# Second row slab's statistics moved to ScalarE, three row slabs loaded ahead of the weights, and the first feed-forward tiles cut into other column widths

## The chip, the cores and the metric

The kernel runs on one core of a Trainium2 chip. The metric is device time in microseconds (us), as a median over runs. Everything that is said of single instructions comes from one profiled execution, which has its own time. TensorE appears in the profile as PE (its weight loads as PEld), VectorE as DVE, ScalarE as ACT, GpSimd as POOL, and the queue that issues the DMAs as SP.

## The reference

`x` is 2048 x 640 in bf16. It is layer-normed, and the result `xn` goes two ways: through a spectral filter (2-D FFT, product with a complex weight, inverse FFT) and through a gated feed-forward network whose output is passed through SiLU. The output is `x + s * g`.

```python
def _layernorm(x, axis=-1, eps=1e-5):
    m = jnp.mean(x, axis=axis, keepdims=True)
    v = jnp.var(x, axis=axis, keepdims=True)
    return (x - m) / jnp.sqrt(v + eps)
...
    def _A_ref(x, w_r, w_i):            # w_r, w_i: 2048 x 321
        X = rfft2(x.astype(jnp.float32)) * (w_r + 1j * w_i)
        return irfft2(X, s=(S, D)).astype(jnp.bfloat16)

    def _B_ref(x, w_gate, w_up, w_down):  # 640 x 1536 twice, 1536 x 640
        return (_gelu(x @ w_gate) * (x @ w_up)) @ w_down

    xn = _layernorm(A_x, axis=-1)
    s = _A_ref(xn, A_w_r, A_w_i)
    g = _silu(_B_ref(xn, B_w_gate, B_w_up, B_w_down))
    return x + s * g
```

## The kernel before, in words

The 2048 rows are dealt into 16 slabs of 128 rows (one row per partition); slab n1 lies in `X[:, n1, :]`. Four slabs make a group g, so a group has 512 columns once it is transposed. The feed-forward network works on groups: the normed slabs are transposed into `xnT[g]` (five chunks of 128 features by 512 rows), and for each of the 12 tiles t of 128 hidden features there is a gate piece and an up piece. A piece (`ffn_piece`, five matmuls, one per chunk) goes into a PSUM bank of its kind: `psg` for gates and `psu` for ups, two banks each, used in turn. A gate is taken out of its bank by a Gelu on ACT into a tile `ge`; an up is taken out by a multiplication with `ge` on DVE into `uT`. After the 12 tiles the product with `w_down` follows (`down_third`). The Fourier stages run as matmuls between these pieces.

Layer norm of a slab takes four steps. `half_stats` (line 174) takes `bn_stats` of each half of the row on DVE, and `bn_aggr` (line 179) joins them to mean and variance. `root` adds epsilon on DVE (line 188) and raises to the power -0.5 on POOL (line 190). `norm` (line 196) subtracts and scales in place on DVE; `norm_parts` does so in two column parts, of 384 and 256 features, so that the first transposes can start sooner. `slab_Tparts` (lines 726 to 730) transposes the two parts on PE and copies each out of PSUM; for slab 0 both copies are on ACT, for slab 1 the second is on DVE. `slab_T` (lines 469 to 473) does a whole slab, with the copy on ACT for slab 2 and on DVE for slab 3.

The order of the work is written out by hand. Every engine takes its instructions in the order of the program. The list `back` holds the feed-forward work, entry by entry, and `plan[s]` holds what is issued behind entry s (`put`). Entries 0 to 2 compute tiles 0 to 2 on slab 0 and then on slab 1, with pieces of 128 columns (`ffn_slab`). Entries 3 to 7 compute tiles 3 to 7 on slabs 0 and 1 together, with 256 columns (`ffn_part` with h = 0), and entries 8 to 15 tiles 0 to 7 on slabs 2 and 3 (h = 1). From entry 16 on pieces have 512 columns (`ffn_half`). Before `back` starts, PE runs warm-up matmuls on constants (`warm_pe`, line 512).

The loads are issued on SP at the very beginning (lines 94 to 108) and are served in this order: slab 0, the gate weights of tiles 0 to 2, slab 1, the up weights of tile 0, those of tiles 1 and 2, slabs 2 and 3 together, then gate and up weights of tiles 3 and 4, of 5 and 6, of 7, and later slabs and weights.

POOL makes integer tables for the Fourier matrices: `vt_iota` (line 221) writes half a table each, and `tinv_phase` (line 308) and `ft_phase` (lines 338 to 342) work on them. `inv_rest` is five tiny DVE instructions on constants; `ft_v` (line 333) is a table row on ACT, one behind each of ten entries.

Of the kernel before, what the change touches and what calls it, by code (L numbers as in the profile page):

```python
# [9 lines left out]
FP32 = mybir.dt.float32  # L10
# [4 lines left out]
P = 128  # L15
# [61 lines left out]
def build(nc, env):  # L77
# [5 lines left out]
    def load_x(n0, n, eng=nc.sync):  # L83
        eng.dma_start(out=X[:, n0:n0 + n, :], in_=xv[:, n0:n0 + n, :])
# [6 lines left out]
        for k in range(2):  # L91
            load_w(k, t0, t1)

    load_x(0, 1)
    load_w(0, 0, 3)
    load_x(1, 1)
    load_w(1, 0, 1)
    load_w(1, 1, 3)
    load_x(2, 2)
    load_gu(3, 5)  # L100
    load_gu(5, 7)
    load_gu(7, 8)
# [82 lines left out]
    def root(n0, n):  # L185
# [6 lines left out]
        for k in range(n):  # L192
            rstd[n0 + k] = r[:, k:k + 1]

    def norm(n1, c0=0, c1_=D):
        nc.vector.tensor_scalar(out=X[:, n1, c0:c1_], in0=X[:, n1, c0:c1_], scalar1=mva[n1 // 4][:, n1 % 4, 0:1],
                                scalar2=rstd[n1], op0=ALU.subtract, op1=ALU.mult)
        if c1_ == D:
            done.add(("n", n1))
# [15 lines left out]
    lint = gtile([LH], INT32)  # L215
    nc.gpsimd.iota(lint, pattern=[[1, LH]], base=0, channel_multiplier=0)
    vt = gtile([NS, P], INT32)

    def vt_iota(h):
        nc.vector.memset(vt[:, 8 * h, 0:1], 0)  # L220
# [80 lines left out]
    vt_iota(0)  # L301
    stats(0)
    root(0, 1)
    inv_consts()

    def tinv_phase(h):
# [356 lines left out]
    def ffn_piece(g, t, k, c0, c1_):  # L663
        new_uT(g)
        for j in range(c0 // P, c1_ // P):
            assert ("T", 4 * g + j) in done
        ps = bank(k)[:, c0:c1_]
        WT = (Wg, Wu)[k]
        for c in range(5):
            nc.tensor.matmul(ps, lhsT=WT[:, c, t * P:(t + 1) * P], rhs=xnT[g][:, c, c0:c1_],  # L670
                             start=(c == 0), stop=(c == 4))
        if k == 0:
            ges[t] = work.tile([P, 512], BF16, tag="ge", bufs=3, name="ge")[:, c0:c1_]
            nc.scalar.activation(out=ges[t], in_=ps, func=ACT.Gelu_apprx_tanh)  # L674
        else:
            nc.vector.tensor_tensor(out=uT[g][:, t, c0:c1_], in0=ps, in1=ges[t], op=ALU.mult)  # L676

    def ffn_part(g, t, h):
        for k in range(2):
# [28 lines left out]
        for t, k in tk:  # L708
            ffn_piece(0, t, k, j * P, j * P + P)

    GG, REST = ((0, 0), (1, 0)), ((0, 1), (2, 0))

    def run(*items):
        for it in items:
# [8 lines left out]
    def slab_Tparts(n1):  # L723
        if n1 == 0:
            xnT[0] = xg.tile([P, 5, 512], BF16, tag="xg", name="xnT0")
        for (a, b), ev in zip(PARTS, (nc.scalar.copy, nc.scalar.copy if n1 == 0 else nc.vector.tensor_copy)):
            pt = psB.tile([P, 5, P], BF16, tag="b")
            for c in range(a, b):
                nc.tensor.transpose(out=pt[:, c, :], in_=X[:, n1, c * P:(c + 1) * P], identity=ident)
            ev(out=xnT[0][:, a:b, n1 * P:n1 * P + P], in_=pt[:, a:b, :])  # L730
        done.add(("T", n1))

    NP = 8
    back = [(run, (ffn_slab, 0, GG), (norm_parts, 1), (vt_iota, 1), (ffn_slab, 0, REST), (slab_Tparts, 1),
             (ffn_slab, 0, ((1, 1), (2, 1))),
             (half_stats, 2, 0)),
            (run, (ffn_slab, 1, GG + REST[:1]), (half_stats, 2, 1), (root, 2, 1), (ffn_slab, 1, REST[1:])),
            (run, (ffn_slab, 1, ((1, 1), (2, 1))), (norm, 2), (stats, 3), (root, 3, 1))]
    for h in range(2):
        for t in range(0 if h else 3, NP):  # L740
            back.append((ffn_part, 0, t, h))
    for g in range(4):
        for t in range(NP if g == 0 else 0, NT):
            for k in range(2):
# [6 lines left out]
    def put(s, *item):  # L751
        plan[s].append(item)

    put(5, norm, 3)
    put(5, slab_T, 2, 1)
    put(6, slab_T, 3, 0)
    for g in range(5):
        put(3 + g, ft_v, g)
        put(8 + g, ft_v, 5 + g)
# [92 lines left out]

    warm_pe(19)
    norm_parts(0)
    stats(1)
    slab_Tparts(0)
    warm_pe(2)
    root(1, 1)
    inv_rest()

    put(5, phase_const)

    for s, b in enumerate(back):
# [34 lines left out]
```

## Time and profile before

| | us |
|---|---|
| median of 3 runs | 207.86 (207.09 to 207.91) |
| profiled execution | 207.12 |
| its span, first to last instruction | 205.3 |
| PE busy in the span | 198.7 (97%) |
| DVE busy | 129.9 (63%) |
| ACT busy | 124.7 (61%) |
| POOL busy | 33.9 (17%) |

The time of the profiled execution is its span and 1.82 us around it. PE is busy nearly throughout, so what counts is the time in which PE has nothing to do and the time that its matmuls take. A matmul's record goes on for a while after the next one has begun, since matmuls are pipelined: the distance between the starts of two pieces tells how long PE needs for one. These distances are 0.28 us for five matmuls of 128 columns, 0.545 us for 256 and 1.08 us for 512 (starts at 9.71 and 9.99, 12.20 and 12.75, 32.67 and 33.75 us). The part of the span that the change touches lies before 27 us.

### The profile page before, as it was taken

To read this page: it belongs to the slowest core of one execution; us is meant where nothing else is said; L and a number is where in the kernel's file an instruction comes from. 1 tells how busy PE (TensorE), PEld (TensorE's weight loads), DVE (VectorE), ACT (ScalarE), POOL (GpSimd) and SP (SyncE) were. 2 spreads that over 40 slices of the span, in tenths; PEclk is the share of its full clock that TensorE was granted. 3 is DMA by queue.
4 is the path that set the end of the run, shared out by engine and by line. 5 is a ranking of instruction groups with operands and counts; after the bars stand their busy time and mean duration, and the time that the engine had idled before them with its cause. 6 is when DMAs were issued, how large, how long until landed. Compare 5 with 4: busy or idle time off the path is not lost.

```text
span 205.3 us, 4412 instructions
## 1 busy us (share of the span) xinstructions
PE 198.7 (97%) x1626; PEld 121.2 (59%) x1643; DVE 129.9 (63%) x357; ACT 124.7 (61%) x230; POOL 33.9 (17%) x61
## 2 busy tenths in 40 slices
PE   7999999999999999999999999999999999999993
PEld 5788855777555555475644444447775555556762
DVE  7886966797678842336565655433568768775653
ACT  2547567767868787225787777424555654656641
POOL 5328688945001100000000000000000000000000
PEclk9999999999999999999999999999999999999998
DMA  5999999899987799289965332369731332242111
GB/s 168 303 305 314 369 291 135 168 146 179 176 161 169 166 186 172 68 198 229 192 137 108 73 67 65 82 139 294 228 86 74 96 123 74 63 132 78 66 51 65
DMA packets 46199, 31.81 MB, mean 155 GB/s; under 512 B 12512, under 2 KB 43872, under 8 KB 46176
## 3 DMA queue, kind: packets, MB, share of 16 engines
q1 hardware_dynamic: 46176, 31.52, 67.1%
q8 instruction: 13, 0.21, 0.5%
q14 instruction: 10, 0.08, 0.1%
HBM read 21.66 MB, written 7.88 MB: 144 GB/s over the span
## 4 chain that ended last, share of the span: by engine, by line
PE 90%; DVE 4%; DMA 2%; issue 1%; ACT 1%; POOL 1%; SPq 0%; DVEq 0%
PE psu L670 24%; PE psg L670 24%; PE psg L694 13%; PE psu L694 12%; PE pd L490 5%; PE pu L552 3%; PE pv L597 2%; PE pz L481 2%; DMA X<-in_A_x_dram 2%; PE pd L494 2%; PE px L532 2%; DVE st L174 1%; DVE uT L676 1%; POOL rst L190 1%; PE pt L326 0%
## 5 line engine op out<-in xcount | busy, mean ns | idle before, releaser
L670 PE MATMUL psu<-xnT,Wu 128*128 128x512 bf16 (+2 forms) x289 | 60.4, 339 | 0.6 <-issue 0.3
L670 PE MATMUL psg<-xnT,Wg 128*128 128x512 bf16 (+2 forms) x284 | 59.9, 338 | 0.8 <-issue 0.3
L676 DVE TENSOR_TENSOR uT<-psu,ge 128x512 bf16<-128x512 f32 (+2 forms) x59 | 34.4, 586 | 33.7 <-PE psu L670 27.4
L674 ACT ACTIVATE ge<-psg 128x512 bf16<-128x512 f32 (+2 forms) x59 | 30.6, 518 | 28.9 <-PE psg L670 27.6
L694 PEld LDWEIGHTS <-uT 128*128 128x128 bf16 x384 | 36.1, 98 | 15.2 <-issue 0.5
L670 PEld LDWEIGHTS <-Wu 128*128 128x128 bf16 x295 | 26.5, 98 | 21.8 <-issue 1.3
L670 PEld LDWEIGHTS <-Wg 128*128 128x128 bf16 x295 | 26.2, 98 | 20.9 <-issue 1.0
L694 PE MATMUL psg<-Wd,uT 128*128 128x320 bf16 (+1 forms) x192 | 30.4, 303 | 0.0
L694 PE MATMUL psu<-Wd,uT 128*128 128x320 bf16 (+1 forms) x192 | 29.6, 296 | 0.0
L539 DVE TENSOR_TENSOR p<-xs,W 128x642 bf16<-128x642 bf16 x32 | 14.4, 492 | 8.9 <-ACT xs L535 8.5
L502 ACT CAST zd<-pd 128x644 bf16<-128x644 f32 x15 | 12.3, 883 | 4.6 <-PE pd L494 4.6
L611 ACT ACTIVATE eo<-pd 128x640 bf16<-128x640 f32 x16 | 10.4, 701 | 7.4 <-PE pd L494 7.4
L599 ACT CAST vs<-pv 128x640 bf16<-128x640 f32 x16 | 11.0, 690 | 6.1 <-PE pv L597 6.1
L174 DVE BATCH_NORM_STATS2 st<-X 128x6 f32<-128x320 bf16 x32 | 14.1, 481 | 0.3 <-issue 0.2
L535 ACT CAST xs<-px 128x642 bf16<-128x642 f32 x16 | 11.1, 692 | 4.0 <-PE px L532 3.6
L620 DVE TENSOR_TENSOR cs<-eo 128x640 bf16<-128x640 bf16 x16 | 7.1, 485 | 7.5 <-ACT eo L611 7.5
L483 ACT CAST Z<-pz 128x640 bf16<-128x640 f32 x16 | 11.0, 694 | 1.1 <-PE pz L481 1.1
L190 POOL TENSOR_TENSOR rst<-ve,mhalf 128x1 f32<-128x1 f32 (+2 forms) x9 | 6.5, 719 | 27.2 <-DVE ve L188 27.2
L645 DVE TENSOR_TENSOR Yall<-Yall,G 128x640 bf16<-128x640 bf16 (+3 forms) x18 | 8.1, 450 | 1.8 <-ACT G L699 1.6
L703 DVE SCALAR_TENSOR_TENSOR G<-th,psg 128x320 bf16<-128x320 f32 x8 | 3.9, 486 | 7.6 <-ACT th L702 7.6
L646 DVE TENSOR_TENSOR Yall<-Yall,xt 128x640 bf16<-128x640 bf16 (+3 forms) x18 | 8.2, 454 | 0.6
L552 PE MATMUL pu<-p,N 64*64 64x321 bf16 x128 | 8.2, 304 | 0.1
(138 smaller groups left out, 213.1 us busy)
## 6 DMA issues: line engine op xcount, KB each, us to landing
ZDR<-zd SPq DMA_DIRECT2D x16, 160.5 KB, 4.2
UDR<-us SPq DMA_DIRECT2D x32, 80.2 KB, 2.6
xt<-in_A_x_dram SPq DMA_DIRECT2D x8, 320.0 KB, 3.2
W<-in_A_w_r_dram SPq DMA_DIRECT2D x14, 160.5 KB, 6.8
W<-in_A_w_i_dram SPq DMA_DIRECT2D x14, 160.5 KB, 5.1
out_dram<-Yall SPq DMA_DIRECT2D x14, 160.0 KB, 1.8
B<-ZDR SPq DMA_DIRECT2D x6, 321.0 KB, 8.4
Vin<-UDR SPq DMA_DIRECT2D x6, 321.0 KB, 5.8
```

Source lines behind the costliest of these rows:

```text
L174: nc.vector.bn_stats(out=st[:, k, :], in_=X[:, n1, 320 * k:320 * k + 320])
L483: nc.scalar.copy(out=Zt[n1], in_=pz)
L502: ev(out=zd.rearrange("p a c (m b) -> p a c m b", b=2)[:, :, :, :, b], in_=pd[b])
L535: nc.scalar.copy(out=xs.rearrange("p (k l) -> p k l", k=2), in_=px[:, :, 0:L])
L539: nc.vector.tensor_tensor(out=pp, in0=xs, in1=WT[:, h].rearrange("p k l -> p (k l)"), op=ALU.mult)
L552: nc.tensor.matmul(pu[64 * lo:64 * lo + 64, hh, 0:L], lhsT=NM[r, kind, 0:64], rhs=pp[r, lo * L:(lo + 1) * L], start=first, stop=not first)
L599: nc.scalar.copy(out=vs, in_=pv)
L611: nc.scalar.activation(out=eo[:, b], in_=py[b], func=ACT.Copy, scale=(2.0 if n0 // 4 in BY_SILU else 1.0) / (S * D))
L670: nc.tensor.matmul(ps, lhsT=WT[:, c, t * P:(t + 1) * P], rhs=xnT[g][:, c, c0:c1_], start=(c == 0), stop=(c == 4))
L674: nc.scalar.activation(out=ges[t], in_=ps, func=ACT.Gelu_apprx_tanh)
L676: nc.vector.tensor_tensor(out=uT[g][:, t, c0:c1_], in0=ps, in1=ges[t], op=ALU.mult)
L694: nc.tensor.matmul(ph, lhsT=uT[g][:, t, j * P:(j + 1) * P], rhs=Wd[:, t, c0:c1_], start=(t == 0), stop=(t == NT - 1))
```

## The change

The loads of slabs 1 and 2 are issued directly after that of slab 0, ahead of all weights, and slab 3 is loaded alone where slabs 2 and 3 were loaded together. The statistics of slab 1 are made on ACT: the row's first element, negated, serves as a shift (`nx`); one activation sums the row and another sums the squares of the shifted row. POOL makes the mean and the square of the shifted mean from them with three tiny instructions, and DVE joins them in one tiny instruction to variance plus epsilon; the root stays on POOL. The squares' unused outputs go to `junk`, which lies in the half of the integer table that `vt_iota(1)` writes later.

The norm of slab 1 and `vt_iota(1)` are issued before `back`, and `inv_rest` behind entry 5. Entry 0 is now three gates of slab 0, the transposes of slab 1 (both copies on ACT), and two ups; entry 1 is three gates and two ups of slab 1, with the statistics of slab 3 and the norm of slab 2 on DVE; entry 2 is the up of tile 2 on both slabs at once with 256 columns; entry 3 is tile 3 on slabs 0 and 1, the transposes of slab 2 and the norm of slab 3; entry 4 is tile 4 on slabs 0 and 1 with the transposes of slab 3 between its gate and its up. Entries 5 to 9 are tiles 0 to 4 on slabs 2 and 3, and entries 10 to 15 are tiles 5 to 7 on all four slabs with 512 columns. The number of entries stays as it was.

```diff
-    load_x(0, 1)
+    for n1 in range(3):
+        load_x(n1, 1)
     load_w(0, 0, 3)
-    load_x(1, 1)
     load_w(1, 0, 1)
     load_w(1, 1, 3)
-    load_x(2, 2)
+    load_x(3, 1)
...
+    def stats_act(n1):
+        nx, s1, s2 = c1("nx"), c1("s1"), c1("s2")
+        xs = X[:, n1, :]
+        nc.scalar.activation(out=nx, in_=X[:, n1, 0:1], func=ACT.Copy, scale=-1.0)
+        nc.scalar.activation(out=junk, in_=xs, func=ACT.Copy, accum_out=s1)
+        nc.scalar.activation(out=junk, in_=xs, func=ACT.Square, bias=nx, accum_out=s2)
+        dm, dq = c1("dm"), c1("dq")
+        nc.gpsimd.tensor_scalar(out=mva[n1 // 4][:, n1 % 4, 0:1], in0=s1, scalar1=1.0 / D, scalar2=0.0, op0=ALU.mult,
+                                op1=ALU.add)
+        nc.gpsimd.tensor_scalar(out=dm, in0=s1, scalar1=1.0 / D, scalar2=nx, op0=ALU.mult, op1=ALU.add)
+        nc.gpsimd.tensor_scalar(out=dq, in0=dm, scalar1=dm, scalar2=-1e-5, op0=ALU.mult, op1=ALU.add)
+        return s2, dq
+
+    def root_act(n1, s2, dq):
+        ve, r = c1("vea"), c1("rsta")
+        nc.vector.scalar_tensor_tensor(out=ve, in0=s2, scalar=1.0 / D, in1=dq, op0=ALU.mult, op1=ALU.subtract)
+        nc.gpsimd.tensor_tensor(out=r, in0=ve, in1=mhalf[:, 0:1], op=ALU.pow)
+        rstd[n1] = r
...
     root(0, 1)
+    sq1 = stats_act(1)
     inv_consts()
...
         if k == 0:
-            ges[t] = work.tile([P, 512], BF16, tag="ge", bufs=3, name="ge")[:, c0:c1_]
-            nc.scalar.activation(out=ges[t], in_=ps, func=ACT.Gelu_apprx_tanh)
+            if c0 != P:
+                ges[t] = work.tile([P, 512], BF16, tag="ge", bufs=3, name="ge")
+            nc.scalar.activation(out=ges[t][:, c0:c1_], in_=ps, func=ACT.Gelu_apprx_tanh)
...
-    GG, REST = ((0, 0), (1, 0)), ((0, 1), (2, 0))
+    GATES, UPS = tuple((t, 0) for t in range(3)), ((0, 1), (1, 1))
...
-        for (a, b), ev in zip(PARTS, (nc.scalar.copy, nc.scalar.copy if n1 == 0 else nc.vector.tensor_copy)):
+        for (a, b), ev in zip(PARTS, (nc.scalar.copy, nc.scalar.copy)):
...
-    back = [(run, (ffn_slab, 0, GG), (norm_parts, 1), (vt_iota, 1), (ffn_slab, 0, REST), (slab_Tparts, 1),
-             (ffn_slab, 0, ((1, 1), (2, 1))),
-             (half_stats, 2, 0)),
-            (run, (ffn_slab, 1, GG + REST[:1]), (half_stats, 2, 1), (root, 2, 1), (ffn_slab, 1, REST[1:])),
-            (run, (ffn_slab, 1, ((1, 1), (2, 1))), (norm, 2), (stats, 3), (root, 3, 1))]
-    for h in range(2):
-        for t in range(0 if h else 3, NP):
-            back.append((ffn_part, 0, t, h))
+    NQ = 5
+    back = [(run, (ffn_slab, 0, GATES), (slab_Tparts, 1), (half_stats, 2, 1), (root, 2, 1), (ffn_slab, 0, UPS)),
+            (run, (ffn_slab, 1, GATES), (half_stats, 3, 0), (ffn_slab, 1, UPS), (norm, 2), (half_stats, 3, 1),
+             (root, 3, 1)),
+            (run, (ffn_piece, 0, 2, 1, 0, 256)),
+            (run, (ffn_part, 0, 3, 0), (slab_T, 2, 1), (norm, 3)),
+            (run, (ffn_piece, 0, 4, 0, 0, 256), (slab_T, 3, 0), (ffn_piece, 0, 4, 1, 0, 256))]
+    for t in range(NQ):
+        back.append((ffn_part, 0, t, 1))
+    for t in range(NQ, NP):
+        for k in range(2):
+            back.append((ffn_half, 0, t, k))
...
-    put(5, norm, 3)
-    put(5, slab_T, 2, 1)
-    put(6, slab_T, 3, 0)
...
     norm_parts(0)
-    stats(1)
+    root_act(1, *sq1)
+    half_stats(2, 0)
     slab_Tparts(0)
     warm_pe(2)
-    root(1, 1)
-    inv_rest()
-
+    norm_parts(1)
+    vt_iota(1)
+
+    put(5, inv_rest)
     put(5, phase_const)
```

More of the change, by code (lines that the diff above doesn't have):

```diff
@@ L217, in build @@
     vt = gtile([NS, P], INT32)
+    junk = vt[:, 8:13, :].rearrange("p n k -> p (n k)").bitcast(FP32)
     def vt_iota(h):
@@ L672, in ffn_piece @@
         if k == 0:
-            ges[t] = work.tile([P, 512], BF16, tag="ge", bufs=3, name="ge")[:, c0:c1_]
-            nc.scalar.activation(out=ges[t], in_=ps, func=ACT.Gelu_apprx_tanh)
+            if c0 != P:
+                ges[t] = work.tile([P, 512], BF16, tag="ge", bufs=3, name="ge")
+            nc.scalar.activation(out=ges[t][:, c0:c1_], in_=ps, func=ACT.Gelu_apprx_tanh)
         else:
-            nc.vector.tensor_tensor(out=uT[g][:, t, c0:c1_], in0=ps, in1=ges[t], op=ALU.mult)
+            nc.vector.tensor_tensor(out=uT[g][:, t, c0:c1_], in0=ps, in1=ges[t][:, c0:c1_], op=ALU.mult)
     def ffn_part(g, t, h):
```

## The prediction

> **What bounds the kernel now.** I read the page first, for whether another engine than PE matters.
>
> ```profile
> PE 198.7 (97%) x1626; PEld 121.2 (59%) x1643; DVE 129.9 (63%) x357; ACT 124.7 (61%) x230; POOL 33.9 (17%) x61
> ...
> PEclk9999999999999999999999999999999999999998
> ```
>
> PE is busy for 97% of the span at full granted clock. So the change can only move the start, where PE has gaps. The chain of waits in order of time, cut to the first 18 us, says what makes them (start, length, what):
>
> ```profile
> 1.64 4.11 DMA X<-in_A_x_dram
> ...
> 5.78 0.90 DVE st L174 x2
> ...
> 7.18 0.58 POOL rst L190
> ...
> 7.78 0.39 DVE X L196
> ...
> 8.22 0.55 PE pt L729 x5
> ...
> 11.47 0.56 POOL rst L190
> ...
> 12.50 0.80 DVE st L174 x2
> ...
> 13.65 0.44 DVE uT L676
> ...
> 14.13 0.71 PE psu L670 x5
> ```
>
> The chain runs over the load of slab 1 (landed at 5.75), its statistics, root and norm, then over DVE's queue, and reaches PE for good at 14.13; behind that PE is dense. The timeline of PE alone gives the gaps (start, length of the records, operation, count):
>
> ```profile
> 6.52 0.82 PE L670 MATMUL psg<-xnT,Wg 128*128 128x128 bf16 x10
> 7.18 0.44 PE L670 MATMUL psu<-xnT,Wu 128*128 128x128 bf16 x5
> 7.46 0.44 PE L670 MATMUL psg<-xnT,Wg 128*128 128x128 bf16 x5
> 8.22 0.54 PE L729 MATMUL pt<-ident,X 128*128 128x128 bf16 x5 [0.32 <-DVE X L196]
> 8.60 0.72 PE L670 MATMUL psu<-xnT,Wu 128*128 128x128 bf16 x10
> ...
> 11.66 0.71 PE L670 MATMUL psu<-xnT,Wu 128*128 128x256 bf16 x5
> ...
> 13.29 0.71 PE L670 MATMUL psg<-xnT,Wg 128*128 128x256 bf16 x5
> 14.13 0.71 PE L670 MATMUL psu<-xnT,Wu 128*128 128x256 bf16 x5
> ...
> 17.45 0.72 PE L670 MATMUL psg<-xnT,Wg 128*128 128x256 bf16 x5
> ```
>
> From 6.52 (first gate) to 17.45 (first gate on slabs 2 and 3), 10.93 us, PE does 12 pieces of 128 columns (0.28 each, 3.36), 10 of 256 (0.545, 5.45) and three slabs' transposes (0.28, 0.84): 9.65. The gaps are 1.28: 0.48 before the transposes at 8.22, 0.23 before 11.66, 0.29 before 14.13, the rest in pieces of 0.1. Last, ACT shows the turnaround of a bank:
>
> ```profile
> 5.99 0.75 ACT L730 COPY xnT<-pt 128x384 bf16<-128x384 bf16 x2 [3.78 <-PE pt L729]
> 7.10 0.56 ACT L674 ACTIVATE ge<-psg 128x128 bf16<-128x128 f32 x2 [0.36 <-PE psg L670]
> ...
> 9.63 0.56 ACT L674 ACTIVATE ge<-psg 128x128 bf16<-128x128 f32 x2 [0.56 <-PE psg L670]
> ```
>
> A gate that starts at 9.15 has its Gelu begin at 9.63: 0.48, that is 0.28 of matmuls and 0.20 behind them. The Gelu takes 0.28, and the bank's next gate starts 0.08 after it (7.38 to 7.46). On DVE it is 0.27 behind the matmuls (ups from 8.60, multiplication at 9.14) and 0.28 for the multiplication. So a bank of 128 columns is back after 0.84 (gate) or 0.91 (up), and with two banks of a kind a third piece of the same kind in a row must wait, unless something else lies between.
>
> **The change, part by part.**
>
> *Loads.* A load lands when the bytes ahead of it have moved. Rows, issue to landing: slab 0 0.72 to 3.0, gates of tiles 0 to 2 1.18 to 5.28, slab 1 1.64 to 5.75, first up weights 2.20 to 6.5, next 2.73 to 8.1, slabs 2 and 3 3.25 to 8.95. Slab 1 is now second: 1.18 + 2.3 (slab 0's own time) = 3.5; slab 2 some 0.5 later. The gate weights have 960 KB to land with them, as the first up weights had: 6.5 at the latest, against the first gate at 6.45 to 6.5; 0.05 at most, taken as 0. First up weights 1120 KB, by bytes between the rows at 6.5 and 8.1: 7.2, needed at 8.1. Next, 1440 KB: 8.5, needed at 8.4; 0.1, which lies in a wait below. Slab 3 (1600 KB) 8.95 as before; tiles 3 and 4 unchanged, landed by 11.2, needed from 11.5 on. SP issues one DMA more (0.4 to 0.6 us), while it is some 6 us ahead of the landings: 0.
>
> *Statistics on ACT.* One tiny activation (0.20, row of line 206) and two over 640 columns, which the trace does not show with a sum. Nearest rows: 0.69 (copy of 640 from PSUM, line 473) and 0.91 (norm on ACT, line 434). I take 0.75, since the first sum is a plain copy; end at 3.55 + 0.20 + 1.50 = 5.25, with 0.91 5.57. Next on ACT are slab 0's copies at 5.99 (row above), so this is hidden with 0.4 to 0.7 us to spare. POOL's three tiny instructions take 0.3 apiece (distances of line 354's row at 33.4 us); behind slab 0's root (ends 4.98) they end by 5.9. DVE joins at 5.95, POOL's root (0.58) ends at 6.8, norm parts of slab 1 0.36 and 0.28: the first part is there at 7.2, against 8.1 before. DVE loses statistics of slab 1 (0.89 + 0.21 + 0.15), `inv_rest` (0.6, from 7.0 to 7.7, now behind entry 5) and a copy (0.29). `vt_iota(1)` (1.01 on POOL) goes from 8.51 to 7.5 and holds slab 2's root until 8.5; that is used at 11: 0. `tinv_phase` starts 1.5 us later, behind `inv_rest`; its first user on PE comes at 38 us: 0. The `ge` tile that the two slabs of a tile now share is written by one engine in the old order: 0.
>
> *PE's order.* This is where I find the cost. First gate 6.5; it waits 0.12 for the second copy of slab 0, as before.
> - Third gate of slab 0: its bank is that of the first, whose Gelu ends at 7.38 (row 7.10, 0.28 each), so it starts at 7.5 as before (7.46). The up that filled the hole (7.18) is gone: gap 0.29. Then the transposes of slab 1 follow at once, at 7.8: the gap of 0.48 is gone.
> - ACT does the third Gelu until 8.25, then both copies (0.75, row 5.99): 9.05. Two ups fill 0.56 until 8.65 (or from the weights' landing, 8.8), three of five chunks of the next gate go after the first copy; gaps 0.29 together. Next gate ends at 9.2.
> - Third gate of slab 1: 0.84 behind the first's start, filled with 0.56: gap 0.29. Before, an up stood in that place (9.71).
> - Up of tile 2, third up in a row: 0.91 after the first, filled with 0.56: gap 0.35. It starts at 11.0, tile 3 at 11.5 and 12.1.
> - Transposes of slab 3 need `norm(3)`, which stands in DVE's queue behind the multiplication of tile 3: up ends 12.6, +0.27 +0.40 +0.42 (row 15.29, 0.44) + 0.08 = 13.75; PE has slab 2's transposes and gate 4 until 13.43: gap 0.31.
> - Their copy (0.28 + 0.27 + 0.48 + 0.08 = 1.11) is awaited by the first gate on slabs 2 and 3; the up of tile 4 fills 0.28 + 0.545: gap 0.28.
>
> Sum of gaps 0.12 + 0.29 + 0.29 + 0.29 + 0.35 + 0.31 + 0.28 = 1.93, against 1.28: **+0.65**. Tiles 5 to 7 with 512 columns: six pieces of 1.08 for twelve of 0.545, -0.06; one 256 for two 128, -0.02. Beyond, both kernels do the same work at the same entries (5 to 9 are 1.09 of PE either way, 10 to 15 are 1.09 against 1.08), and PE is dense (8.75 of 8.75 us in the stretch from 17.45 to 26.2), so cheaper evictions there buy nothing and the shift is carried to the end. Net **+0.57, taken as 0.6**: the profiled execution's 207.12 becomes 207.7; it stood 0.74 below the median, so against the median **208.5**. Some 0.5% (1.04 us) is what a measurement of this kernel can tell from no change; 0.6 is inside. Each gap is sure to about 0.05, so this case's own range is 208.3 to 208.9.
>
> **Rivals.**
> - *Late inputs (slower).* If ACT's sums end after 5.99, they delay slab 0's copies and all behind. It decides from landing + 0.2 + two sums = 5.99: with 0.91 a landing after 3.97, with 0.69 after 4.41. Slab 1 may land as late as 1.18 + 4.1 (its own former time) = 5.28, which with 0.91 costs 1.3; a sum may cost more than any row. The middle (4.4, 0.91) costs 0.4. Up weights at 9.0 in place of 8.5 cost another 0.4, and up weights of tile 3 (landing 11.2, needed at 12.1) whatever they pass 12.1 by. In total 1.0 to 1.9: 208.9 to 209.8, point 209.2. For it: 480 KB now stand before the first weights.
> - *Banks turn around in time (faster).* The long chain above loses its first links, and DVE some 2 us of work ahead of 14 us. If two pieces of 128 columns covered a turnaround, only the 0.12 would be left: 1.28 - 0.12 + 0.08 = 1.2 gained, 206.6. It decides at a turnaround of 0.56; the rows say 0.84 and 0.91.
> - *DVE in time for slab 3 (no change).* If `norm(3)` gets in front of the last two gaps (ready by 13.4), 0.59 of the sum goes: 207.9.
> - *The clock.* In the trace the 19 warm-up matmuls of 256 columns took 4.23 us, 0.22 each, against 0.109 later: PE starts at half rate though the record says 1.00. If the new gaps brought that back for as long as the warm-up needed (4.2 us of work at half rate), 2.1 us would be added: 210.6. Against it: before has gaps of 0.48 in the same place at full rate, and mine are at most 0.35. The Trainium skill (TensorE: Matmul & The Clock Gate, "A second HAM failure mode: psum-queue depth-cycling") says that small idles between groups of matmuls, when banks are cycled, make the clock swing between half and full rate; by that rule this rival would be the forecast, by the rows above it is not.
>
> **Numbers.** My sum 0.43; late inputs 0.36; faster 0.08; no change 0.10; clock 0.03. Slower by over 0.5%: 0.30 of late inputs, the clock and 0.05 of the first case's tail, 0.38. Faster 0.08. Within: 0.54. The range leaves out the faster case, the clock and the tip of late inputs: 207.4 to 209.7.
>
> **What would show it.** In the new profile: statistics on ACT ending before slab 0's copies at about 6.0; first gate at 6.5; transposes of slab 1 at 7.8; gaps on PE before the third gate of each slab, before the up of tile 2, the transposes of slab 3 and the first gate on slabs 2 and 3 at 14.8; DVE no longer on the chain. At 14.24 that gate would mean no change (17.45, less the 3.21 by which tiles 5 to 7 on four slabs, still to come, outlast those on two). The prediction is wrong if it comes before 14.0 or after 15.3, or if the time is won or lost behind it.

## The result, and the profile after

| | before | after |
|---|---|---|
| median | 207.28 us (207.08 to 208.68, 8 runs) | 209.34 us (208.46 to 210.16, 8 runs) |
| profiled execution | 207.12 us | 209.71 us |
| its span | 205.3 us | 207.9 us |

The ratio is 1.0093, with a 95% interval from 1.0074 to 1.0113: the change costs 0.9%, about 2 us, where 0.6 us was forecast. The three runs in the table ahead of the prediction are the first three of these eight. Ratios compare fast runs only, so one run of `e5_alternate` (211.64 us) is not in its ratio.

In three of the eight runs of the changed kernel, the profiled one among them, the mean granted clock of TensorE (the share of its full clock that the profile says it was given) is 0.992, in the other five it is 1.00. These five have a median of 208.92 and the three 209.87, so something that happens in some runs only costs about 1 us, and something that happens in all of them the rest. One of the five took 209.71, so the clock is not all that varies.

The page of the changed kernel shows the same picture as before, with PE busy for 96% of the span. Only the beginning differs, in the clock (granted clock in 40 slices of the span, in tenths):

```profile
PEclk9799999999999999999999999999999999999999
```

The second digit is a 7: between 5.2 and 10.4 us the clock was not full. The chain of waits in order of time (start, length, what) gives the places. Line numbers of the changed kernel are up to 22 higher than before (691 is 670, 698 is 676, 215 is 196):

```profile
2.10 5.24 DMA Wg<-in_B_w_gate_dram
...
14.99 0.44 DVE X L215
...
29.58 1.53 POOL rst L190
...
32.44 0.58 ACT ge L696
33.06 0.38 PE psg L691
```

The chain now starts with the load of the first gate weights. Statistics and norm of slab 1 are gone from it, as forecast. Two other things are new: DVE's norm of slab 3 (14.99) ahead of its transposes, where DVE was to be off the chain, and, far behind the changed part, a stretch over DVE, the root on POOL (29.58) and a late Gelu (32.44) before a gate at 33.06. The timeline of PE alone (start, length of the records, operation, count, in brackets the idle time and its releaser) gives the start of each piece:

```profile
7.38 1.59 PE L691 MATMUL psg<-xnT,Wg 128*128 128x128 bf16 x15 [1.13 <-DMA Wg<-in_B_w_gate_dram]
...
12.65 0.70 PE L691 MATMUL psu<-xnT,Wu 128*128 128x256 bf16 x5 [0.17 <-DVE uT L698]
...
15.47 0.45 PE L490 MATMUL pt<-ident,X 128*128 128x128 bf16 x5 [0.20 <-DVE X L215]
...
16.51 0.72 PE L691 MATMUL psg<-xnT,Wg 128*128 128x256 bf16 x5
```

The first gate starts at 7.38, where it was 6.52 before, after 1.13 us in which PE did nothing. The first gate on slabs 2 and 3 starts at 16.51, against 14.24 for no change. Two measures of a gap are used below. A bracket counts from the end of the last record, which runs on for some 0.17 after the next piece could start; a gap by the distance of the starts is longer by that (0.34 for the bracket of 0.17 before 12.65).

The windows (start and end, length, then busy time of PE, PEld, DVE, ACT, POOL with counts, granted clock, DMA share, GB/s) say what lies between. Before the change, for comparison:

```profile
3.00:4.50 1.50, 1.50 (x9) 1.06 (x8) 1.43 (x11) 0.00 (x0) 1.11 (x2) 1.00 0.91 289
```

and the changed kernel:

```profile
3.00:4.50 1.50, 1.50 (x10) 1.10 (x9) 1.43 (x10) 1.01 (x4) 1.07 (x2) 1.00 0.67 118
4.50:7.34 2.84, 1.15 (x11) 0.49 (x8) 2.13 (x13) 1.58 (x4) 1.90 (x5) 1.00 1.07 299
7.60:11.05 3.45, 3.45 (x37) 3.45 (x35) 1.28 (x6) 1.58 (x5) 1.53 (x2) 0.51 1.15 305
```

Three readings. In 3.0 to 4.5 us the DMA engines move 118 GB/s; before the change they moved 289 GB/s in the same stretch. In 4.5 to 7.34 us PE is busy for 1.15 of 2.84 us. And from about 7.6 to 11.05 us the granted clock is 0.51, full again behind it. ACT's timeline shows the new statistics:

```profile
3.57 0.72 ACT L199 ACTIVATE GEN<-X 128x640 f32<-128x640 bf16 x1
4.19 0.19 ACT L199 ACTIVATION_READ_ACCUMULATOR GEN<-X 128x1 f32 x1
4.41 0.83 ACT L200 ACTIVATE GEN<-X,nx 128x640 f32<-128x640 bf16 x1
```

The half rate shows there too: the Gelus of the first two gates start 0.53 apart (7.95 and 8.48), because a gate of 128 columns now takes some 0.54 us on PE instead of 0.28. The two sums take 0.72 and 0.83, and each is followed by an instruction of 0.19 that reads the accumulator. The second of these readings ends at 5.33, and the copies of slab 0 follow on ACT at 5.87.

*Where 2.6 us of span went.* The steps are read at three instructions of PE: the first gate, the first gate on slabs 2 and 3, the first product with `w_down`.

- First gate 6.52 to 7.38: **0.86**, the late gate weights.
- From there to the first gate on slabs 2 and 3 took 9.13. No change would have been 7.72 (14.24 less 6.52). The same kernel at full clock, from the same late start, took 7.94 (experiment `e3_warm` below: 7.57 to 15.51). So the half clock cost **1.19** and the order of the pieces **0.22**.
- From there to the first product with `w_down` took 21.03 (16.51 to 37.54). Before it was 17.54 (17.45 to 34.99), and with the 3.21 of tiles 5 to 7 this makes 20.75. The difference of **0.28** is the gap before 33.06.
- From there to the end it is 170.36, against 170.31 before: **0.05**.

The sum is 2.60, the difference of the spans. Without the half clock it is 1.41; the median of the five runs at full clock is 1.64 above that of the kernel before. The 0.86 is the figure of this one execution: two other kernels with the same order of loads (`e2_phase_early`, `e4_loads_only`) started the first gate at 6.83 and 6.64.

*The gap at 33.06.* Rows of DVE's timeline in the changed kernel, the integer masks (line 334) and `ve`, the input of the root of slabs 4 to 7:

```profile
26.05 1.62 DVE L334 TENSOR_SCALAR GEN<-GEN,andm,orm 128x1024 int32<-128x1024 int32 x1
...
29.33 0.17 DVE L188 TENSOR_SCALAR ve<-mva 128x4 f32<-128x4 f32 x1
```

and POOL's timeline in the same stretch:

```profile
25.50 1.61 POOL L363 TENSOR_TENSOR GEN<-GEN 128x805 f32<-128x805 f32 x1
29.58 1.53 POOL L190 TENSOR_TENSOR rst<-ve,mhalf 128x4 f32<-128x4 f32 x1 [2.47 <-DVE ve L188]
```

Before the change the first mask and this root were

```profile
23.77 0.81 DVE L313 TENSOR_SCALAR GEN<-GEN,andm,orm 128x1024 int32<-128x1024 int32 x1
```

```profile
26.23 1.04 POOL L190 TENSOR_TENSOR rst<-ve,mhalf 128x4 f32<-128x4 f32 x1 [2.29 <-DVE ve L188]
```

POOL's tables wait for `phase_const` on DVE, which now starts at 18.81 and started at 15.64 before, 3.17 earlier. The first mask comes only 2.28 later (26.05 against 23.77). Of the 0.9 by which the tables fall behind the mask, 0.6 is `inv_rest`, which now stands directly ahead of `phase_const` (18.22 to 18.81). So the last table (25.50) is running when the first mask starts at 26.05, and that mask takes 1.62 instead of 0.81. Everything behind it on DVE is later, and `ve` comes directly ahead of the second mask (29.41, 0.81). The root then takes 1.53, where it took 1.04, and ends at 31.1 instead of 27.3, 1.6 more than the 2.3 by which the work around it is later. The norms on ACT that wait for it (0.92 each, from 31.61) now stand in the way of a Gelu, whose bank the gate at 33.06 needs.

### The profile page after: what moved, and what is told of

It reads as the page before. It is cut to its first block, busy times and chain, and to the rows that moved or that the text cites. A ratio compares the mean times of both kernels' runs of the same rounds, so it can differ in the third digit from the quotient of the medians.

```text
span 207.9 us, 4334 instructions
## 1 busy us (share of the span) xinstructions
PE 199.4 (96%) x1590; PEld 119.2 (57%) x1608; DVE 129.5 (62%) x349; ACT 126.1 (61%) x233; POOL 35.1 (17%) x64
## 4 chain that ended last, share of the span: by engine, by line
PE 88%; DVE 3%; DMA 3%; issue 2%; ACT 1%; POOL 1%; SPq 1%; DVEq 0%; ACTq 0%
PE psg L691 24%; PE psu L691 23%; PE psg L716 13%; PE psu L716 11%; PE pd L511 4%; PE pu L573 3%; DMA Wg<-in_B_w_gate_dram 3%; PE pv L618 2%; PE pz L502 2%; PE pd L515 2%; PE px L553 2%; DVE uT L698 1%; POOL rst L190 1%; SPq L84 1%; DVE st L174 1%
## 5 line engine op out<-in xcount | busy, mean ns | idle before, releaser
L698 DVE TENSOR_TENSOR uT<-psu,ge 128x512 bf16<-128x512 f32 (+2 forms) x55 | 33.9, 619 | 36.3 <-PE psu L691 28.3
L696 ACT ACTIVATE ge<-psg 128x512 bf16<-128x512 f32 (+2 forms) x56 | 30.0, 536 | 30.4 <-PE psg L691 29.9
L691 PEld LDWEIGHTS <-Wg 128*128 128x128 bf16 x280 | 25.5, 101 | 24.1 <-DMA Wg<-in_B_w_gate_dram 1.4
L691 PEld LDWEIGHTS <-Wu 128*128 128x128 bf16 x275 | 25.2, 99 | 23.0 <-issue 1.1
L632 ACT ACTIVATE eo<-pd 128x640 bf16<-128x640 f32 x16 | 10.4, 701 | 7.4 <-PE pd L515 7.4
L174 DVE BATCH_NORM_STATS2 st<-X 128x6 f32<-128x320 bf16 x30 | 13.3, 480 | 0.0
L190 POOL TENSOR_TENSOR rst<-ve,mhalf 128x2 f32<-128x2 f32 (+2 forms) x8 | 6.4, 796 | 26.6 <-DVE ve L188 26.6
```

The lines of the kernel that those rows point to most:

```text
L174: nc.vector.bn_stats(out=st[:, k, :], in_=X[:, n1, 320 * k:320 * k + 320])
L632: nc.scalar.activation(out=eo[:, b], in_=py[b], func=ACT.Copy, scale=(2.0 if n0 // 4 in BY_SILU else 1.0) / (S * D))
L696: nc.scalar.activation(out=ges[t][:, c0:c1_], in_=ps, func=ACT.Gelu_apprx_tanh)
```

## The experiments

Ratios are to the kernel before, with 95% intervals, from runs on the same chip. Gate weights here means those of tiles 0 to 2.

### Gate weights third in the order of the loads (`e1_gate_weights_third`)

```diff
-    for n1 in range(3):
+    for n1 in range(2):
         load_x(n1, 1)
     load_w(0, 0, 3)
+    load_x(2, 1)
     load_w(1, 0, 1)
...
     root_act(1, *sq1)
-    half_stats(2, 0)
     slab_Tparts(0)
     warm_pe(2)
     norm_parts(1)
+    half_stats(2, 0)
     vt_iota(1)
```

> The changed kernel with the gate weights of tiles 0 to 2 loaded third, ahead of slab 2, and slab 2's first half of statistics behind the norm of slab 1. Theory (the weights' landing sets the first gate: 7.34 us in the changed kernel's profile against 5.28 before): they are issued some 0.5 us earlier with 160 KB less ahead, land at about 6.5 to 6.8, and the first gate starts at 6.6 to 6.8 in place of 7.38; PE's idle stretch before it shrinks from 1.13 to 0.3 to 0.5 us and the clock stays full more often. Time 0.6 to 1.4 us below the changed kernel's 209.3, so 207.9 to 208.7. Rival (only the order of the pieces on PE costs): the first gate moves but the time stays within 0.3 us of 209.3.

Measured: 208.29 us against 207.15, 1.0056 (1.0042 to 1.0070); the granted clock is 1.00 or 0.998 in all runs. PE's timeline:

```profile
6.75 1.26 PE L692 MATMUL psg<-xnT,Wg 128*128 128x128 bf16 x15 [0.27 <-ACT xnT L753]
...
8.95 0.45 PE L692 MATMUL psu<-xnT,Wu 128*128 128x128 bf16 x5 [0.39 <-DMA Wu<-in_B_w_up_dram]
...
15.09 0.72 PE L692 MATMUL psg<-xnT,Wg 128*128 128x256 bf16 x5
```

The gate weights land at 6.74 and PE has no gap of a microsecond. None of the four runs has the slow clock, and the excess over the kernel before falls from 2.06 to 1.14 us, as expected. The short gaps between pieces are all still there (0.35 before the up of tile 2 at 11.22, 0.38 before the transposes at 14.05), so they do not bring the half clock. But the kernel is still 0.6% slower than before. From the first gate to the first gate on slabs 2 and 3 it takes 8.34, against 7.72 for no change. Of this difference 0.55 is a new wait before the second up of slab 0: it starts at 8.95, 0.83 behind the first where 0.28 would do, since the up weights of tiles 1 and 2 land at 8.91 (issued at 3.15). The prediction had put them at 8.5.

### More warm-up matmuls (`e3_warm`)

```diff
-    warm_pe(2)
+    warm_pe(12)
```

> The changed kernel with 12 in place of 2 warm-up matmuls of 256 columns between the transposes of slab 0 and the first gate; they fill PE's idle stretch of 1.13 us before the late gate weights (10 x 0.109 = 1.09 us) and should delay nothing. Theory (in some runs the idle stretch lets the clock fall to half from 7.6 to 11.1 us, which costs 0.8 us): granted clock 1.0 in every run, the pieces from 7.4 on at 0.28 us each, no run of 209.7 and above; median 0.4 to 0.9 below 209.3, so 208.4 to 208.9. Rival (the clock's dip is chance, or has no part in the median): the same spread of clocks and times, median within 0.3 of 209.3.

Measured: 208.94 us, 1.0086 (1.0072 to 1.0100). The loads are those of the changed kernel, and ten more matmuls on constants fill the wait for the weights. Windows, columns as above:

```profile
4.50:7.34 2.84, 2.76 (x20) 1.94 (x19) 2.13 (x13) 1.59 (x4) 1.89 (x5) 1.00 1.07 299
7.60:11.05 3.45, 3.28 (x53) 2.95 (x51) 1.59 (x6) 2.15 (x8) 1.53 (x2) 1.00 1.16 304
```

PE is busy for 2.76 of the 2.84 us, the clock stays at 1.00 (0.997 at least in every run), and the weights are as late as without the extra work (the DMA engines move 152 GB/s in 3.0 to 4.5 us). The first gate comes at 7.57, 0.19 later than without the extra work; the first gate on slabs 2 and 3 at 15.51 instead of 16.51. Idle time of PE in front of the first gate is what halves the clock: with it filled here, or gone in `e1_gate_weights_third`, none of ten runs shows the dip, where three of eight did. (At a chance of 3 in 8 for each run, ten in a row without it would come about once in a hundred.) The median says little: the excess falls from 2.06 to 1.79 us only, and the two intervals overlap, because without the extra matmuls the dip strikes in some runs only. One run of 210.13 us, the profiled one, was not expected; its span is 207.0, like that of the others, so what it lost lies outside the span.

### The loads alone (`e4_loads_only`), and the order alone (`e11_order_alone`)

The kernel before, with nothing changed but the order of the loads (x of slabs 0, 1 and 2 first, then weights, slab 3 alone):

```diff
-    load_x(0, 1)
+    for n1 in range(3):
+        load_x(n1, 1)
     load_w(0, 0, 3)
-    load_x(1, 1)
     load_w(1, 0, 1)
     load_w(1, 1, 3)
-    load_x(2, 2)
+    load_x(3, 1)
```

> The kernel before with the new order of loads alone: slabs 0, 1, 2, then the weights, slab 3 alone. Theory (the late gate weights are the largest part of the loss): they land at about 7.3 and the first gate starts there, 0.85 later than before's 6.52; slab 1's statistics are ready earlier on DVE, so its transposes wait no longer and 0.4 to 0.5 us come back; 0.3 to 0.6 us above before, and 0.8 more where the clock dips: 207.6 to 208.7. Rival (loads are hidden, order of the pieces costs): within 0.2 of before's 207.3.

Measured: 207.64 us, 1.0020 (1.0008 to 1.0032). The gate weights land 4.5 us after their issue at 2.10, at 6.6 and not at the expected 7.3, and the first gate starts at 6.64. The first gate on slabs 2 and 3 starts at 17.32, 0.13 earlier than before, so in the profiled run the start is not slower. That run is the fastest of the ten; others have spans up to 1.0 longer than its 205.3, and what is late in those was not traced.

The changed kernel, with the loads of before and the statistics of slab 1 back on DVE:

```diff
-    for n1 in range(3):
-        load_x(n1, 1)
+    load_x(0, 1)
     load_w(0, 0, 3)
+    load_x(1, 1)
     load_w(1, 0, 1)
     load_w(1, 1, 3)
-    load_x(3, 1)
+    load_x(2, 2)
...
-    back = [(run, (ffn_slab, 0, GATES), (slab_Tparts, 1), (half_stats, 2, 1), (root, 2, 1), (ffn_slab, 0, UPS)),
+    back = [(run, (ffn_slab, 0, GATES), (slab_Tparts, 1), (ffn_slab, 0, UPS), (stats, 2), (root, 2, 1)),
...
-    root_act(1, *sq1)
-    half_stats(2, 0)
+    stats(1)
     slab_Tparts(0)
     warm_pe(2)
+    root(1, 1)
```

> The new order of the pieces alone: before's loads, statistics of slab 1 on DVE as before, those of slab 2 behind the two ups of slab 0; the rest as in the changed kernel. Theory (the order costs some 0.6 us by itself and the masks 0.3): first gate at 6.5, granted clock full in every run, gaps before the third gates, the up of tile 2 and the transposes of slab 3, the piece at about 31 us held by the norms; 0.8 to 1.3 us above before, 208.0 to 208.5. Rival (only the late weights and the clock cost): within 0.3 of before's 207.2.

Measured: 208.56 us, 1.0070 (1.0056 to 1.0084). PE's timeline:

```profile
11.36 0.71 PE L690 MATMUL psu<-xnT,Wu 128*128 128x256 bf16 x5 [0.55 <-DVE uT L697]
```

The order of the pieces alone costs 1.4 us in the median. From the first gate (6.35) to the first gate on slabs 2 and 3 (15.14) it takes 8.79, 1.07 more than the 7.72 of no change. With DVE's statistics the transposes of slab 1 wait until 7.98, and the up of tile 2 waits 0.55 (before 11.36) since the multiplications that empty its banks stand behind the statistics of slab 2. The gap around 33 us is in it too (21.01 from 15.14 to the first product at 36.15). The two halves, 0.0020 and 0.0070, make 0.0090 of the 0.0093. That does not mean that the ACT statistics, which are in neither, are worth nothing: the late first gate of the profiled run and the half clock are in neither half, too. The stretch between the two gates shows what the statistics do in the new order. It takes 8.79 here, with DVE's statistics, and 7.94 in `e3_warm` with those of ACT and the loads that go with them. So some 0.8 is gained there, and the late weights and the half clock take more than that.

### The old order of pieces with statistics on ACT (`e9_old_order`)

The changed kernel with the gate weights third, the entries of before (the second copy of slab 1 is on DVE again), and `inv_rest` behind `phase_const` of entry 5:

```diff
-    back = [(run, (ffn_slab, 0, GATES), (slab_Tparts, 1), (half_stats, 2, 1), (root, 2, 1), (ffn_slab, 0, UPS)),
+    back = [(run, (ffn_slab, 0, GG), (ffn_slab, 0, REST), (slab_Tparts, 1),
+             (ffn_slab, 0, ((1, 1), (2, 1))),
+             (half_stats, 2, 0)),
...
+    for h in range(2):
+        for t in range(0 if h else 3, NP):
+            back.append((ffn_part, 0, t, h))
...
-    half_stats(2, 0)
...
-    put(5, inv_rest)
     put(5, phase_const)
+    put(5, inv_rest)
```

> The statistics of slab 1 on ACT without the new order of the pieces: before's entries and tile widths, before's place of the masks, the loads of e1 (slab 0, slab 1, gate weights, slab 2, up weights, slab 3), norm of slab 1 and vt_iota(1) early, inv_rest behind phase_const at entry 5. Theory (what costs is the late weights and the new order, and the statistics by themselves are a gain): the first gate starts at 6.4 to 6.8 (6.52 before), the gap of 0.48 before slab 1's transposes goes and DVE's two waits of 0.23 and 0.29 shrink; the first gate on slabs 2 and 3 comes 0.2 to 0.8 us earlier than before's 17.45; 206.5 to 207.1, a little faster than before. Rival (DVE or the up weights take the gain back): 207.2 to 207.8, with a gap before the second up of slab 0.

Measured: 207.72 us, 1.0027 (1.0015 to 1.0038). The gap of 0.48 before the transposes of slab 1 is gone: they start at 7.90. But the pieces around them now wait for up weights (0.16 before 7.33 and 0.18 before 8.35), and DVE's two waits before 11.42 and 13.89 are as they were. So the gain is spent before 14 us. A new wait of 0.31 stands before 17.65, and its cause is a row of DVE's timeline:

```profile
16.03 0.83 DVE L267 SCALAR_TENSOR_TENSOR o_r<-l_r,cq 128x1 f32<-128x1 f32 x1
```

The tiny instruction at 16.03 normally takes 0.15. POOL's first integer table (two instructions, 2.37 from 15.66) was running, and the tiny one ended at 16.86, just when the first of these two ended (15.66 and half of 2.37 is 16.85). The copy of slab 3 at 17.12 stood behind it.

### Tables of POOL earlier (`e2_phase_early`), and masks later (`e6_masks_later`)

Both try to remove the gap before 33.06. The first issues `phase_const` before `back` starts, in the changed kernel:

```diff
-    put(5, phase_const)
+    phase_const()
```

> The changed kernel with the one DVE instruction that POOL's table work waits for (phase_const) issued before the feed-forward work in place of behind entry 5. Theory (POOL's tables, started 3 us later than before, collide with DVE's two masks, one mask takes 1.62 us in place of 0.81, the root of slabs 4 to 7 takes 1.53 in place of 1.04, and a Gelu waits behind the norms on ACT): tinv_phase starts at about 15 in place of 19.1, ft_phase some 1.2 us earlier, both masks take 0.81, and the gap of 0.3 us on PE before the piece at 33.06 goes; time 0.2 to 0.4 below 209.3. Rival (POOL is off the path): no difference, within 0.15.

Measured: 209.54 us, 1.0110 (1.0096 to 1.0124), no better. The masks, in their old places, take 0.76 and 0.81, and the gap at 33 is gone: from the first gate on slabs 2 and 3 (15.81) to the first product (36.55) it takes 20.74. But PE waits 1.25 before slab 3's transposes, at full clock. A row each of PE, DVE and POOL in this kernel:

```profile
14.77 0.45 PE L490 MATMUL pt<-ident,X 128*128 128x128 bf16 x5 [1.25 <-DVE X L215]
```

```profile
13.38 1.33 DVE L215 TENSOR_SCALAR X<-X,mva,rst 128x640 bf16<-128x640 bf16 x1
```

```profile
13.35 2.43 POOL L329 TENSOR_SCALAR GEN<-GEN,u,ph_t 128x1024 int32<-128x1024 int32 x2
```

The norm of slab 3 takes 1.33 instead of 0.44, while POOL runs its table. The collision was moved from a place with slack to one that PE waits for.

The second is `e1_gate_weights_third` with the two masks behind entries 14 and 16 instead of 12 and 14:

```diff
-    put(12, tinv_mask, 0)
-    put(14, tinv_mask, 1)
+    put(14, tinv_mask, 0)
+    put(16, tinv_mask, 1)
```

> The kernel of e1 with the two masks on DVE (tinv_mask) two entries later, behind entries 14 and 16. Theory (DVE's mask and POOL's work on the tables or the root exclude each other, and the masks stand right where the root of slabs 4 to 7 needs DVE and POOL): the mask that took 1.6 us takes 0.8, the root takes 0.6 to 1.1 in place of 1.53, and the gap of 0.28 on PE at about 31.6 goes; 208.0. Rival (the gap is the norms' own length on ACT): the gap stays, 208.3.

Measured: 208.13 us, 1.0039 (1.0024 to 1.0054). From the first gate on slabs 2 and 3 (14.55) to the first product (35.28) it takes 20.73, as before the change (20.75), and 0.30 less than in `e1_gate_weights_third` (21.03). POOL's root:

```profile
26.61 2.00 POOL L191 TENSOR_TENSOR rst<-ve,mhalf 128x4 f32<-128x4 f32 x1 [1.45 <-DVE ve L189]
```

The mask runs at its full speed (0.81 from 26.44). The root is even longer (2.00), with a mask directly behind its input, but its input `ve` comes at 26.36 instead of 27.91, so the norms on ACT are out of the Gelu's way. The median alone would not tell this kernel from `e1_gate_weights_third` (the intervals overlap); the traces do. That stretch takes 21.01 to 21.04 in all six kernels with the new order in which a mask meets the last table, and 20.73 or 20.74 in the four in which it does not. In `e2_phase_early` the masks did not move, only the tables, so it is the meeting that costs the 0.28.

### Gates and ups in turn (`e5_alternate`, `e10_alternate_masks`), and statistics of slab 3 earlier (`e7_stats3_early`)

On `e1_gate_weights_third`, slab 1 in the order gate, gate, up, gate, up, so that a turnaround of a bank is covered:

```diff
-            (run, (ffn_slab, 1, GATES), (half_stats, 3, 0), (ffn_slab, 1, UPS), (norm, 2), (half_stats, 3, 1),
-             (root, 3, 1)),
+            (run, (ffn_slab, 1, ((0, 0), (1, 0), (0, 1), (2, 0))), (half_stats, 3, 0), (ffn_slab, 1, ((1, 1),)), (norm, 2),
+             (half_stats, 3, 1), (root, 3, 1)),
```

> The kernel of e1 (gate weights loaded third; 208.29 us) with the pieces of slab 1 in the order of the kernel before: gate, gate, up, gate, up in place of three gates and two ups. Theory (a bank of 128 columns comes back after 0.84 us for a gate and 0.91 for an up, so a third of a kind in a row costs 0.29 and 0.35): both gaps go, on PE from the first gate of slab 1 to the up of tile 2 takes 1.45 to 1.5 us in place of 1.98; 0.3 to 0.6 us gained, 207.7 to 208.0. Rival (the gaps are given back by the later wait for norm(3)): no gain, 208.3, and the gap before slab 3's transposes grows by as much.

Measured: 208.09 us, 1.0038 (1.0025 to 1.0052). Five of the six runs took 207.72 to 208.37, the profiled one 211.64. Its trace shows a second case of the half clock, far from any late weights. A row of PE's timeline and two windows:

```profile
54.35 1.24 PE L692 MATMUL psg<-xnT,Wg 128*128 128x512 bf16 x4 [1.98 <-DMA xnT<-X]
```

```profile
51.51:54.35 2.84, 0.86 (x18) 0.55 (x16) 2.06 (x5) 2.37 (x3) 0.00 (x0) 1.00 0.65 164
55.65:59.05 3.40, 3.40 (x16) 1.68 (x14) 0.86 (x2) 1.50 (x3) 0.00 (x0) 0.50 1.06 194
```

The first gate of the second group waits 1.98 for slabs that are transposed by DMA. PE is busy for 0.86 of the 2.84 us before it, and 1.3 us later the clock is at half for 3.40 us.

The same edit with the later masks of above:

> e5 and e6 together on the kernel of e1. Theory (the gaps of the third pieces and the masks are separate and add up): 0.2 and 0.15 below e1's 208.29, so 207.8 to 208.0. Rival (one hides the other): 208.1.

Measured: 208.26 us, 1.0039 (1.0023 to 1.0054). The medians of the two edits apart and together cannot be told from one another, so no sum of gains shows. Four of the nine runs took 207.23 to 207.75 and five 208.26 to 208.82; the profiled one is the slowest. In its timeline the gate of tile 3 starts at 10.99, 1.99 behind the second slab's first gate (9.00), against 2.52 in `e1_gate_weights_third` (9.24 to 11.76): 0.53 gained. But the transposes of slab 3 wait for its norm 0.65 (from 12.92, when the gate of tile 4 is through, to 13.57) instead of 0.38, which gives 0.27 back. And at 53.24 the first gate of the second group waits 1.09 for its DMA transposes, at full clock; before the change the corresponding gate started at 51.80 without a wait. That is not the price of an earlier start: `e6_masks_later` and `e8_together` reach the first gate on slabs 2 and 3 as early (14.55 and 14.66, here 14.61) and do not wait. Why the transposes are late in the two profiled runs with this order, and whether they are in the others, stays open.

The other way is the norm of slab 3 earlier. On `e1_gate_weights_third`, its statistics and root were put ahead of the ups of slab 1:

```diff
-            (run, (ffn_slab, 1, GATES), (half_stats, 3, 0), (ffn_slab, 1, UPS), (norm, 2), (half_stats, 3, 1),
-             (root, 3, 1)),
+            (run, (ffn_slab, 1, GATES), (stats, 3), (root, 3, 1), (ffn_slab, 1, UPS), (norm, 2)),
```

> The kernel of e1 with all of slab 3's statistics and its root ahead of the two ups of slab 1, where DVE idles for 0.9 us, in place of half of them behind norm(2). Theory (the transposes of slab 3 wait for norm(3), which waits for the root): the root ends 1.5 us earlier, norm(3) follows the multiplication of tile 3 at once, and the gap before the transposes falls from 0.38 to about 0.1 to 0.2; 0.1 to 0.3 gained, 208.0 to 208.2. Rival (the multiplication of tile 3 itself is the last to end): gap and time stay, 208.3.

Measured: 208.96 us, 1.0080 (1.0067 to 1.0093): worse. The gap before slab 3's transposes shrinks from 0.38 to 0.29, but the multiplications of slab 1's ups start at 11.12 only, and the up of tile 2 waits 0.66 for them (until 11.46), where it waited 0.17. DVE takes its instructions in order, and neither place tried for these statistics, before or behind the ups, is one that nobody waits for.

### All of it together (`e8_together`)

The alternating order, the later masks and the early statistics of slab 3 in one kernel, with slabs 1 and 2 loaded over ACT's queue beside slab 0 and the gate weights on SP's (the edit of the loads alone is shown):

```diff
-    for n1 in range(3):
-        load_x(n1, 1)
+    load_x(0, 1)
+    load_x(1, 1, nc.scalar)
     load_w(0, 0, 3)
+    load_x(2, 1, nc.scalar)
     load_w(1, 0, 1)
```

> e5, e6 and e7 together, and slabs 1 and 2 loaded over ACT's own DMA queue, so that the weights keep their place in SP's queue. Theory (late weights, three kinds of waits and the masks are all of the loss against before): the first gate starts at 6.4 to 6.6 and the loss is gone, 206.5 to 207.3, as fast as before or up to 0.6 us faster. Rival (something else costs too): 207.6 or more.

Measured: 208.69 us, 1.0069 (1.0050 to 1.0088): a miss. Slab 0 lands 2.78 after its issue instead of 2.3, with two more slabs on the way beside it, and the first gate comes at 6.89. The first gate on slabs 2 and 3 comes at 14.66, still 0.42 behind no change. The profiled run (208.11) is the fastest of the six; what the others lose was not traced.

No version was faster than the kernel before.

## Why the prediction was right and where it was wrong

The direction of the likeliest case was right, its size was not: +0.6 was forecast, and +2.1 measured. That the median of 209.34 lies inside the range of 207.4 to 209.7 is luck. It stands at the place of the late-inputs rival (208.9 to 209.8), outside the likeliest case's own range of 208.3 to 208.9. And the range was set from a median of 207.86 for the kernel before, from which its upper end is 1.8 away; from the 207.28 of eight runs the change is 2.06.

By its own signs the prediction was wrong. The first gate on slabs 2 and 3 was to come at 14.8, and not after 15.3; it came at 16.51, and at full clock still at 15.51 (`e3_warm`). DVE was to leave the chain and is on it at 14.99. Time was lost behind that gate, too: 0.28.

**Loads: the step that failed.** The step was "6.5 at the latest, against the first gate at 6.45 to 6.5; 0.05 at most, taken as 0". They landed at 7.34, and the first gate was 0.86 late. The step took a load to land when the bytes ahead of it have moved, at the rate of the rows before. But the weights were issued at 2.10 instead of 1.18, and in 3.0 to 4.5 us the DMA engines moved 118 GB/s instead of 289: the slabs ahead were nearly through and the weights had hardly begun. The packets in the trace say so (1280 bytes for a slab's row, 768 for these weights): at 4.5 us 16 of slab 2's 128 were still to start and 38 of the weights' 640 had started; before the change it was 603 of 640. 1.5 us at 171 GB/s less is 257 KB, which at 289 GB/s takes 0.89 us, and that is about what 7.34 is over 6.5. This sum is rough: by it the 195 GB/s of `e4_loads_only` would give 7.0, and there they landed at 6.6. Nor is 7.34 fixed; the four kernels with this order of loads have 6.6, 6.8, 7.3 and 7.34, all later than "6.5 at the latest". The up weights came late as well. The first were put at 7.2 and landed at 8.1, which nobody waited for; the next were put at 8.5 and landed at 9.1, and at 8.91 in `e1_gate_weights_third`, where PE waited 0.55 for them. Why a load of weights begins so late after its issue was not measured apart.

**The clock: a rival rejected by the wrong gap.** The rival said 2.1 us if the clock halved, and was given 0.03, since "before has gaps of 0.48 in the same place at full rate, and mine are at most 0.35". The gaps that I had counted did not bring it back, as `e1_gate_weights_third` and `e11_order_alone` show (gaps up to 0.55, clock full). A gap that I had not counted did: 1.13 us ahead of the first gate, with PE busy 40% of the 2.84 us before it. It cost 1.19 in the profiled run and struck in three of eight. `e5_alternate` has the second case, behind 1.98 us at 54.35. The length of one gap does not decide: `e2_phase_early` has one of 1.25 at full clock. The busy share separates the traces. PE is busy for as little as 1.10 of some 2.84 us in the changed kernel and 0.81 in `e5_alternate`; behind the warm-up and ahead of the last microseconds, no such stretch of the other eleven traces has less than 1.55. Why five of eight runs of the changed kernel escaped is open; they were not traced. This rival hung on the loads' step, and its chance should have been tied to that step's. The Trainium skill (TensorE: Matmul & The Clock Gate, "What's actually happening") gives the clock's window as 3413 ns; the stretches of half clock here, 3.45 and 3.40 us, agree with it. The Trainium skill's rule on the same page ("HAM oscillation — how this bites in real kernels"), to have no idle gaps over some 3.4 us, is too lax here, where 1.13 us in a half-idle stretch were enough. The bank-cycling rule that the prediction quoted as this rival's support was not what happened.

**The order of pieces: right in kind, too large.** Forecast were gaps of 1.93 against 1.28, +0.57 net. At full clock from a late start (`e3_warm`) the net cost is 0.22, and from an early start in `e6_masks_later` 0.32 (8.04 from 6.51 to 14.55, against 7.72), with 0.16 of a wait for up weights in it. Both have ACT's statistics; with DVE's (`e11_order_alone`) it is 1.07. Single gaps in the changed kernel: 0.34 before the up of tile 2 (forecast 0.35), 0.37 before slab 3's transposes (0.31), 0.21 before the first gate on slabs 2 and 3 (0.28). The 0.12 before the second half of the first gate is gone, since the second copy has long been made when the gate is late, and the transposes of slab 1 with the gates of slab 1 lose 0.41 in `e3_warm` instead of 0.58.

**ACT's statistics: right.** Slab 1 was to land at 3.5 and did at 3.46; the sums were put at 0.75 apiece and took 0.72 and 0.83; the end was to be 5.25 and is 5.33. They are hidden by 0.54 us, which rules out late sums, the main part of the late-inputs rival. Its total came out only because another load was late.

**The later tables: costed at nothing, worth 0.28.** The step was "`tinv_phase` starts 1.5 us later, behind `inv_rest`; its first user on PE comes at 38 us: 0". It started 3.1 us later, and the step asked only who waits for its result, and not who shares its time: DVE's masks. The rule was there to be read. The Trainium skill (SBUF — State Buffer, "SBUF: two separate sides") says that DVE and GpSimd share one pair of ports, held by one instruction until its end, if DVE's is of a fast form, or reads two operands from SBUF while GpSimd's reads SBUF too. Four rows here agree: a mask of 1.62 for 0.81, a norm of 1.33 for 0.44, a tiny instruction of 0.83 for 0.15 that ended with POOL's, and a root on POOL of 1.53 and 2.00 for 1.04.

**Behind 17.45**: forecast was that the shift is carried unchanged to the end. But for the 0.28 this holds (0.05). The rival in which banks turn around in time, the only faster one, is out: the waits of 0.34 and 0.35 for banks are there in every version with three pieces of a kind in a row. In the new order DVE was never in time for slab 3, not even where its statistics were put first (a gap of 0.29).

## What to carry to other kernels

When loads are put in another order, ask for each what the DMA engines move between its issue and its first data, and let the landing of a load in a new position range over all rows seen, not over bytes alone. A wait at the start of a kernel can cost more than its own length, through the clock: tie the two chances together, or fill the wait with matmuls. And an instruction on DVE or POOL that moves in time needs a look at what the other of the two runs then, even if nobody is waiting for its result.

## What was unexpected of the hardware

- The clock halved for 3.45 us after 1.13 us of idle time, with PE busy 1.15 of the 2.84 us before, and in `e5_alternate` for 3.40 us after 1.98, with 0.86 of 2.84. A longer gap than the first, 1.25 us in `e2_phase_early`, did not bring it about (1.60 of 2.84), nor did 1.09 in `e10_alternate_masks` (1.76 of 2.84). The share of busy time fits all four, the length of the gap does not; a threshold was not measured.
- A sum on ACT costs a second instruction of 0.19 us that reads the accumulator.
- A DVE instruction that starts while POOL's runs can be lengthened by most of the time that POOL's still has to go: 0.81 of 1.06 (the mask), 0.89 of 1.18 (the norm), 0.68 of 0.82 (an instruction of one element per partition, 0.83 instead of 0.15). Not every one is: `bn_stats` (0.87 for two at 20.41 in the changed kernel) and the multiplications (0.42) run beside the tables at their usual length.
- The same load in the same position landed between 4.5 and 5.24 us after its issue, in kernels that do not differ ahead of it on the DMA engines. This alone moves the first gate by 0.7 us from one profiled run to the next (6.64 to 7.38).
